# Two weight units ahead of the first slot, the first loads in another order, and part of the weight scaling on GpSimd

## The chip, the cores and the metric

The kernel runs on one core of a Trainium2 chip. The metric is device microseconds of that core for one execution, lower is better, given as the median of several runs. Engines are named as in the profile: PE (TensorE), DVE (VectorE), ACT (ScalarE), POOL (GpSimd) and SP (SyncE, which here only issues DMAs). Each works through its own instructions strictly in the order in which the program lists them, so an instruction that waits holds up everything behind it on its engine.

## What is computed

Top-k attention (576 tokens, 8 batches, 8 heads of 64), then a two-layer network with an exact GELU:

```python
def _attn_ref(q, k, v):
    top_k = 32
    scores = scale * np.matmul(q, k.transpose(0, 1, 3, 2))
    kth = np.partition(scores, -top_k, axis=-1)[..., -top_k:-top_k + 1]
    scores = np.where(scores >= kth, scores, -1000000000.0)
    scores = scores - np.max(scores, axis=-1, keepdims=True)
    attn = np.exp(scores)
    attn = attn / (np.sum(attn, axis=-1, keepdims=True) + 1e-09)
    return np.matmul(attn, v)

def _moe_ref(x, w_in, w_out):          # x: 4608 x 512, w_in: 512 x 2048, w_out: 2048 x 512
    h = x @ w_in
    g = 0.5 * h * (1.0 + erf(h / np.sqrt(2)))
    return g @ w_out
```

The arrays q, k, v are 32-bit floats; w_in and w_out arrive as 64-bit floats, and the kernel turns their bits into 32-bit floats itself.

## The kernel before

**Slots.** The attention is cut into 144 items, each 128 query rows for two heads (or the 64 tail rows of four heads). A loop over `n` (L617) runs 144 slots and a few more to drain. Slot n gives each engine work on several items at once: PE computes the scores of item n+2 (`scores`), the product with V of item n-3 (`attend`), the transposes of item n-2 (`transposes`) and up to seven or eight pieces of the network (`mlp`); ACT copies scores out of PSUM, runs the two activations of the softmax of item n-1 for each half (`softmax`), and copies PE's results; DVE finds the 32 largest scores of item n (`top_k`: 8 MAX8 and 6 MATCH_REPLACE8), ends with the reciprocal of the softmax sum of item n-1 (`inverse`), and does some normalisations. T0, T1, ... below are the times at which DVE starts the first MAX8 of slot 0, 1, ... .

**Two short chains through POOL tie the engines together.** After `top_k(n)`, `threshold(n)` (L339, L342) makes from the found values what the softmax of item n needs. When ACT has finished the softmax, `add_small` (L356) makes `den`, which DVE's reciprocal L350 waits for at the end of the next slot. `normalise` (L376) then multiplies the two halves of an item's scores by that reciprocal, on POOL or DVE; PE's transposes of the next slot need the result.

**Weights.** The 1 MB of each of 16 units (`ORDER`) is loaded as raw words into a part of `w_out_sb` that is not yet in use, or into a `stage` tile, and turned into 32-bit floats in one slot: ACT runs L175, L177 and (for some) the scaling L179 at the end of the slot before (`weights_size`), POOL runs the scaling L191 (for the others) and the two integer additions L194 and L195 at the top of the slot (`weights_add`), ahead of `add_small` in POOL's order. One unit is made in each of slots 1 to 15 and the last in slot 17. `on_pool` says who scales: ACT for slots 1 to 8, POOL from slot 9 (`START`). `normalise` at the end of slot n is split by the unit of slot n+1: with a unit that ACT scales, DVE takes one of the two halves; with one that POOL scales, both; with none, POOL takes both. A load waits until POOL has finished with the unit that used the buffer before.

**The start.** Memsets and the identity for the transposes come first, then the loads of k and q for the first two pairs of heads (k of pair 0 from ACT's and POOL's queues, all else from SP's), then the loads of the units of slots 1 and 2. PE runs 16 matmuls (`WARM`, L596) while it waits, then transposes q and k of pairs 0 and 1 (`transpose_qk`, L232, copies L236) and computes the scores of items 0 and 1, whose copies (L281, L282) DVE waits for at T0.

**The network** can start only when the first 256 tokens have all heads, which is in slot 9; item 7 (`HASTE`) is hurried through in slot 8 for that. From there pieces are handed out per slot (seven in slots 10 to 16, else eight), and what is left when the 144 slots end is done by PE alone. The next tokens become ready in slot 18.

Of the kernel before, what the change touches and what calls it, by code (L numbers as in the profile page):

```python
# [14 lines left out]
def kernel(  # L15
# [26 lines left out]
    P = 128  # L42
# [27 lines left out]

    raws = {n: [const.tile([P, NJ, 2, D], f32, name=f"raw_{n}{i}") for i in range(m)]
            for n, m in (("k", 2), ("q", 2), ("v", NP + 1))}
    for n, ts in raws.items():
        for t in ts[: 1 if n == "v" else 2]:
            (nc.vector if n == "v" else nc.gpsimd).memset(t[:, NM], 0.0)
    make_identity(nc, ident)
    for t in raws["v"][1:]:
        nc.gpsimd.memset(t[:, NM], 0.0)


    n_pairs = B * NP
# [5 lines left out]
    def load(n, pair, queue=None, queue2=None):  # L87
        if pair >= n_pairs:
            return
        queue = queue or nc.sync  # L90
        queue2 = queue2 or queue
        b, h0 = pair // NP, 2 * (pair % NP)
        t, src = raw_of(n, pair), sources[n]
        for e in range(2):
            queue.dma_start(
                out=t[:, 0:NM, e, :], in_=src[b, h0 + e, 0:SM].rearrange("(t p) d -> p t d", p=P)
            )
            queue2.dma_start(out=t[e * TL : (e + 1) * TL, NM, e, :], in_=src[b, h0 + e, SM:S])

# [18 lines left out]


    ORDER = [0, 1, 2, 3, 8, 9, 4, 5, 10, 11, 6, 7, 12, 13, 14, 15]
    FIRST = 1
    START = 2 * NP + 1
    HASTE = 2 * NP - 1
    WARM = 16
    words = {}
    low = const.tile([P, 1], f32, name="low")
    nc.gpsimd.memset(low, -EXP0 * 2.0**19)
# [1 line left out]
    nc.gpsimd.memset(high, EXP0 * 2.0**-21)  # L131


    SLOT_OF = {u: FIRST + i + (i == UNITS - 1) for i, u in enumerate(ORDER)}
    UNIT_IN = {n: u for u, n in SLOT_OF.items()}
    unit_in = UNIT_IN.get

    def load_weights(n, queue=None):

        queue = queue or nc.sync  # L140
        u = unit_in(n)
        if u is None:
            return
        src, r, c, dst = weights_of(u)
        if src.dtype == f32:
            for x in range(2):
                queue.dma_start(
                    out=dst[:, x], in_=src[(r + x) * P : (r + x + 1) * P, c : c + WS]
                )
            return  # L150


        half, i = src.bitcast(u16), ORDER.index(u)
        if i not in (12, 14, 15):
            at = FT // 2 + 4 * (i % 2)
            t = w_out_sb[:, at : at + 4, :].rearrange("p (a b) n -> p a (b n)", a=2)
        else:
            t = stage.tile([P, 2, 2 * WS], f32, tag="words", name="words")
        for a in range(2):
            queue.dma_start(  # L160
                out=t[:, a].bitcast(u16)[:, 0 : 4 * WS - 1],
                in_=half[(r + a) * P : (r + a + 1) * P, 4 * c + 1 : 4 * (c + WS)],
            )
        words[u] = t
# [15 lines left out]

    def on_pool(u):

        return SLOT_OF[u] >= START

    made = set()

    def weights_add(u):
        if u in words:
            w, _, below, d = parts(u)
            if on_pool(u):  # L190
                nc.gpsimd.tensor_scalar(  # L191
                    w.bitcast(i32), w.bitcast(u32), 2.0**-13, None, op0=ALU.mult
                )
            nc.gpsimd.tensor_tensor(d, d, below, op=ALU.add)  # L194
            nc.gpsimd.tensor_tensor(d, d, w.bitcast(i32), op=ALU.add)  # L195
        made.add(u)


    items, starts = [], []
# [50 lines left out]
    def spread(t, step, n):  # L250

        return bass.AP(tensor=t.tensor, offset=t.offset, ap=[list(t.ap[0]), [step, 2], [1, n]])
# [10 lines left out]
    def scores(i):  # L263
        if i >= N:
            return
        pair, t = items[i]
        S_of[i] = s = work.tile([P, 2 * S], f32, tag="s", bufs=5, name="s")
        s_ps = ps.tile([P, 2, 512], f32, tag="s", bufs=1, name="s_ps")
        t_ps = ps.tile([P, 512], f32, tag="tp", name="t_ps")
        if t < NM:  # L270
            qk = qk_of[pair]
            lhsT = qk[:, t * P : (t + 1) * P]
            nc.tensor.matmul(t_ps[:, 0:P], lhsT=lhsT, rhs=qk[:, SM + P : KT], start=True, stop=True)  # L273
            for c in range(2):
                for e in range(2):
                    rows = slice(e * D, (e + 1) * D)
                    nc.tensor.matmul(  # L277
                        s_ps[:, e, c * 256 : (c + 1) * 256], lhsT=lhsT[rows, :],
                        rhs=qk[rows, KT + c * 256 : KT + (c + 1) * 256], start=True, stop=True,
                    )  # L280
            nc.scalar.activation(spread(s, S + TL, SM), s_ps, func=AF.Copy, scale=scale)  # L281
            nc.scalar.activation(s[:, SM : S + TL], t_ps[:, 0:P], func=AF.Copy, scale=scale)  # L282
        else:
            for r in range(2):
                qk = qk_of[pair + r]
                for e in range(2):
                    nc.tensor.matmul(  # L287
                        t_ps[half(r, e), r * TL : (r + 1) * TL],
                        lhsT=qk[:, SM + e * TL : SM + (e + 1) * TL],
                        rhs=qk[:, SM + P + e * TL : SM + P + (e + 1) * TL],  # L290
                        start=True, stop=True,
                    )

            for r in range(2):
                qk = qk_of[pair + r]
                for e in range(2):
                    rows = slice(e * D, (e + 1) * D)
                    nc.tensor.matmul(  # L298
                        s_ps[half(r, e), r, :], lhsT=qk[rows, SM + e * TL : SM + (e + 1) * TL],
                        rhs=qk[rows, KT:], start=True, stop=True,  # L300
                    )
            s2 = s.rearrange("p (r n) -> p r n", r=2)
            nc.scalar.activation(s2[:, :, 0:SM], s_ps, func=AF.Copy, scale=scale)
            nc.scalar.activation(
                s2[:, :, SM:S], t_ps[:, 0:P].rearrange("p (r n) -> p r n", r=2),
                func=AF.Copy, scale=scale,
            )
# [274 lines left out]
    staging = ExitStack()  # L582
    stage = staging.enter_context(tc.tile_pool(name="stage", bufs=1))

    load("k", 0, nc.scalar, nc.gpsimd)
    load("q", 0)
    load("k", 1)
    load("q", 1)
    for n in range(2):
        load_weights(FIRST + n)  # L590


    idle = raws["v"][0][:, NM].rearrange("p e d -> p (e d)")
# [3 lines left out]
    for pair in range(2):  # L597
        for piece in transpose_qk(pair, pair == 0):
            piece()
        if pair == 0:  # L600
            scores(0)
            scores(1)

# [11 lines left out]
    for n in range(ahead):  # L617

        left[0] = 7 if START < n < START + 2 * NP else 8
        weights_add(unit_in(n))  # L620
        scores(n + 2)

        product = attend(HASTE) if n - 2 == HASTE else n - 3 != HASTE and attend(n - 3)
        late = n > START
        mlp(1)
        tr = transposes(n - 2) if n - 2 != HASTE else []
        if product and n > START and done[0] < len(pieces) and pieces[done[0]][0] > ready[0]:

            for piece in tr[:1]:
                piece()  # L630
            tr, ready[0] = tr[1:], n_tok[0]
        softmax(n - 1, 0)
        mlp(1)
        if not late:
            softmax(n - 1, 1)
        mlp(1)
        prep = prep_in.pop(n, [])
        if len(prep) > 1 and len(tr) == 3:
            tr, prep = tr[:1] + prep[:1] + tr[1:], prep[1:]
        for piece in tr[:-1]:  # L640
            piece()
            ready[0] = n_tok[0]
            mlp(1)
        ready[0] = n_tok[0]
        if late:
            softmax(n - 1, 1)
        if n - 1 != HASTE:
            add_small(n - 1)
        for piece in tr[-1:] + prep:
            piece()  # L650
            mlp(1)

        run_gelus()
        mlp(left[0])
        run_gelus()
        if n - 1 == HASTE:

            def hasty():
                st = stat_of[HASTE]
                nc.vector.tensor_scalar(st["den"], st["den"], 1e-9, None, op0=ALU.add)  # L660
                inverse(HASTE)
                normalise(HASTE, 2)

            top_k(n, {1: hasty})
            for piece in transposes(HASTE):
                piece()
        elif n < N:
            top_k(n, {3: lambda: inverse(n - 1)})
        else:
            inverse(n - 1)  # L670
        threshold(n)
        u = unit_in(n + 1)

        if n - 1 != HASTE:
            normalise(n - 1, 0 if u not in words else 2 if on_pool(u) else 1)

        weights_size(unit_in(n + 1))
        if n >= FIRST:
            load_weights(n + 2)
        if n <= NP:  # L680
            load("v", n)

# [37 lines left out]
```

## Time and profile before

| | |
|---|---|
| median of 9 runs | 1652.05 us (1651.38 to 1652.72) |
| the profiled execution: its own time | 1651.6 us |
| its span, from the first to the last instruction | 1649.8 us |
| busy, PE / DVE / ACT / POOL | 1589.5 / 1421.1 / 1183.3 / 651.1 us |
| mean granted PE clock | 0.980 of full speed |
| T0, T1, T2, T3 | 11.80, 21.46, 31.73, 42.00 us |
| T8, T9, T13, T14 | 93.49, 105.48, 148.55, 159.33 us |
| T15, T16, T17, T18 | 172.94, 182.65, 194.39, 205.22 us |
| first matmul of the network (L496) | 109.08 us |

A page of the profile gives busy times over the whole span; a table by windows gives, for each stretch of time, the length and the busy time of PE, of its weight loads, of DVE, ACT and POOL (with the number of instructions), the granted PE clock, the DMA share and GB/s. A timeline row has the start in us, the duration in us, engine, line, operation, what is written from what, and in brackets how long the engine was idle before it and what ended that.

### The profile page before, as it was taken

To read this page: it belongs to the slowest core of one execution; us is meant where nothing else is said; L and a number is where in the kernel's file an instruction comes from. 1 tells how busy PE (TensorE), PEld (TensorE's weight loads), DVE (VectorE), ACT (ScalarE), POOL (GpSimd) and SP (SyncE) were. 2 spreads that over 40 slices of the span, in tenths; PEclk is the share of its full clock that TensorE was granted. 3 is DMA by queue.
4 is the path that set the end of the run, shared out by engine and by line. 5 is a ranking of instruction groups with operands and counts; after the bars stand their busy time and mean duration, and the time that the engine had idled before them with its cause. 6 is when DMAs were issued, how large, how long until landed. Compare 5 with 4: busy or idle time off the path is not lost.

```text
span 1649.8 us, 25054 instructions
## 1 busy us (share of the span) xinstructions
PE 1589.5 (96%) x8832; PEld 1078.0 (65%) x8832; DVE 1421.1 (86%) x3051; ACT 1183.3 (72%) x2130; POOL 651.1 (39%) x755
## 2 busy tenths in 40 slices
PE   6579799999999999999999999999999999999999
PEld 4355476766666667776666667676666666666665
DVE  7999899988899889998989988998889888999800
ACT  6889767777777777777777777777777777777720
POOL 3678633333333333333333333333333333333300
PEclk8789999999999999999999999999999999999999
DMA  6424110011101111011100111001110001000000
GB/s 171 142 91 131 55 43 1 14 29 33 46 1 28 30 30 28 1 28 36 30 28 5 39 30 43 1 14 28 44 35 1 27 16 35 2 13 6 2 13 13
DMA packets 126621, 56.14 MB, mean 34 GB/s; under 512 B 117760, under 2 KB 117792, under 8 KB 126496
## 3 DMA queue, kind: packets, MB, share of 16 engines
q1 hardware_dynamic: 125376, 54.25, 12.3%
q8 instruction: 70, 1.15, 0.3%
q14 instruction: 55, 0.45, 0.1%
q10 hardware_dynamic: 1056, 0.26, 0.1%
q0 software_dynamic: 64, 0.03, 0.0%
HBM read 45.08 MB, written 9.44 MB: 33 GB/s over the span
## 4 chain that ended last, share of the span: by engine, by line
PE 91%; DVE 5%; ACT 2%; issue 0%; POOL 0%; DVEq 0%; ACTq 0%; POOLq 0%
PE h_ps L496 30%; PE y_ps L532 30%; PE o L444 8%; PE s_ps L277 8%; PE tp L413 7%; DVE top L324 3%; DVE rest L327 2%; PE tp_qk L232 2%; PE t_ps L273 2%; PE o L455 1%; PE s_ps L298 1%; PE tp_t L395 1%; ACT s L364 0%; PE t_ps L287 0%; ACT s L363 0%
## 5 line engine op out<-in xcount | busy, mean ns | idle before, releaser
L324 DVE MAX8 top<-rest 128x8 f32<-128x576 f32 x864 | 609.2, 746 | 0.0
L496 PE MATMUL h_ps<-xT,w_in_sb 128*128 128x256 f32 (+1 forms) x2560 | 552.6, 361 | 3.8 <-ACT g L507 3.8
L532 PE MATMUL y_ps<-w_out_sb,g 128*128 128x512 f32 x1152 | 549.4, 599 | 0.0
L496 PEld LDWEIGHTS h_ps<-xT,w_in_sb 128*128 128x128 f32 x2560 | 428.6, 191 | 67.2 <-issue 20.0
L376 POOL TENSOR_SCALAR s<-s,rden 128x576 f32<-128x576 f32 x265 | 454.3, 1723 | 0.4 <-DVE rden L350 0.4
L327 DVE MATCH_REPLACE8 rest<-top,rest 128x576 f32<-128x576 f32 x576 | 423.2, 742 | 0.0
L356 POOL TENSOR_SCALAR den<-den 128x2 f32<-128x2 f32 x143 | 31.7, 222 | 831.4 <-ACT s L364 830.7
L532 PEld LDWEIGHTS y_ps<-w_out_sb,g 128*128 128x128 f32 x1152 | 195.0, 190 | 166.1 <-issue 164.8
L281 ACT ACTIVATE s<-s_ps 128x1024 f32<-128x1024 f32 x128 | 131.4, 1027 | 168.1 <-PE s_ps L277 146.6
L364 ACT ACTIVATE s<-s,bias 128x576 f32<-128x576 f32 x288 | 223.3, 775 | 12.7
L363 ACT ACTIVATE s<-s,neg 128x576 f32<-128x576 f32 x288 | 224.0, 778 | 0.3 <-POOL neg L339 0.2
L413 PEld LDWEIGHTS tp<-ident,s 128*128 128x128 f32 x1152 | 146.2, 144 | 113.5 <-issue 58.7
L420 ACT COPY pt<-tp 128x512 f32<-128x512 f32 x256 | 147.1, 575 | 102.1 <-PE tp L413 102.0
L327 DVE MATCH_REPLACE8 rest<-top,s 128x576 f32<-128x576 f32 x288 | 211.7, 742 | 0.0
L324 DVE MAX8 top<-s 128x8 f32<-128x576 f32 x288 | 201.7, 742 | 3.9 <-ACT s L282 3.9
L413 PE MATMUL tp<-ident,s 128*128 128x128 f32 x1152 | 178.8, 279 | 26.4 <-ACT pt L396 19.9
L444 PE MATMUL o<-pt,raw_v 128*64 128x256 f32 x1280 | 155.5, 390 | 0.0
L277 PE MATMUL s_ps<-qk 64*128 64x256 f32 x1024 | 152.6, 419 | 0.7 <-ACT s L281 0.7
L350 DVE RECIPROCAL rden<-den 128x2 f32<-128x2 f32 x144 | 23.0, 160 | 138.1 <-POOL den L356 137.6
L444 PEld LDWEIGHTS o<-pt,raw_v 128*64 128x64 f32 x1280 | 87.8, 139 | 66.4 <-issue 24.2
L277 PEld LDWEIGHTS s_ps<-qk 64*128 64x128 f32 x1024 | 92.1, 194 | 23.8 <-issue 1.8
L507 ACT ACTIVATE g<-h_ps 128x512 f32<-128x512 f32 x144 | 78.6, 595 | 33.6 <-PE h_ps L496 32.9
(67 smaller groups left out, 1088.3 us busy)
## 6 DMA issues: line engine op xcount, KB each, us to landing
raw_q<-in_q_dram SPq DMA_DIRECT2D x64, 128.0 KB, 2.4
raw_v<-in_v_dram SPq DMA_DIRECT2D x64, 128.0 KB, 2.4
out_dram<-y SPq DMA_DIRECT2D x32, 256.0 KB, 2.1
w_out_sb<-in_moe_w_in_dram SPq DMA_DIRECT2D x16, 511.8 KB, 4.9
raw_k<-in_k_dram SPq DMA_DIRECT2D x62, 128.0 KB, 2.5
w_out_sb<-in_moe_w_out_dram SPq DMA_DIRECT2D x10, 511.8 KB, 4.1
words<-in_moe_w_out_dram SPq DMA_DIRECT2D x6, 511.8 KB, 4.5
raw_q<-in_q_dram SPq DMA_DIRECT2D x64, 16.0 KB, 2.2
```

The lines of the kernel that those rows point to most:

```text
L277: nc.tensor.matmul(s_ps[:, e, c * 256 : (c + 1) * 256], lhsT=lhsT[rows, :], rhs=qk[rows, KT + c * 256 : KT + (c + 1) * 256], start=True, s ...
L281: nc.scalar.activation(spread(s, S + TL, SM), s_ps, func=AF.Copy, scale=scale)
L324: nc.vector.max(st["top"][:, e, 8 * r : 8 * r + 8], cur[e])
L327: nc.vector.match_replace(rest[:, e], st["top"][:, e, 8 * r : 8 * r + 8], cur[e], LOWEST)
L363: nc.scalar.activation(s, s, func=AF.Prelu, bias=st["neg"][:, e, 1:2], scale=1.0, alpha=STEEP)
L364: nc.scalar.activation(s, s, func=AF.Exp, bias=st["bias"][:, e : e + 1], scale=1.0, accum_out=st["den"][:, e : e + 1],)
L376: (nc.vector if e >= 2 - on_dve else nc.gpsimd).tensor_scalar(s, s, st["rden"][:, e : e + 1], None, op0=ALU.mult)
L413: nc.tensor.transpose(tp[:, j * P : (j + 1) * P], s[:, first + j * P : first + (j + 1) * P], ident)
L420: nc.scalar.copy(out=dst, in_=tp.rearrange("p (j n) -> p j n", j=NM))
L444: nc.tensor.matmul(o[e * D : (e + 1) * D, 0:n], lhsT=vt[:, j, e, :], rhs=pt[:, e * NM + j if j < NM else 2 * NM, :], start=(j == 0), stop= ...
L496: nc.tensor.matmul(h_tile(u)[:, i, :], lhsT=w_in_sb[:, ko, f * P : (f + 1) * P], rhs=xT[:, ko, c0 : c0 + n], start=(ko == 0), stop=(ko == ...
L532: nc.tensor.matmul(y_of[sub], lhsT=g_of[u][:, i, sub * P : (sub + 1) * P], rhs=w_out_sb[:, f, :], start=(f == 0), stop=(f == FT - 1),)
```

## The change

- SLOT_OF: the first two units of ORDER are made in slot 0, the third in slot 1, and so on to the fifteenth in slot 13; the last is made in slot 15. Every unit but the first is two slots earlier than before, the first one slot.
- Three units are loaded before the loop instead of two; the third unit's words get a stage tile of their own. `weights_size` of the two units of slot 0 runs before the loop.
- on_pool: POOL scales in odd slots too (1, 3, 5, 7); ACT scales in slots 0, 2, 4, 6, 8.
- normalise: ahead of a unit that ACT scales, POOL takes both halves; ahead of one that POOL scales before slot 9, DVE takes one; from slot 9 on, both, as before. Ahead of slot 14 (no unit any more) and slot 17 POOL takes both where DVE took both.
- The second integer addition of a unit is taken out of weights_add and comes after add_small in POOL's order (weights_end).
- The start: DVE does most memsets, the loads of k and q of pair 0 are listed before the identity, WARM is 9 instead of 16, and the scores of item 0 are copied out of PSUM by ACT and DVE in three parts instead of two activations on ACT.

```diff
     raws = {n: [const.tile([P, NJ, 2, D], f32, name=f"raw_{n}{i}") for i in range(m)]
             for n, m in (("k", 2), ("q", 2), ("v", NP + 1))}
-    for n, ts in raws.items():
-        for t in ts[: 1 if n == "v" else 2]:
-            (nc.vector if n == "v" else nc.gpsimd).memset(t[:, NM], 0.0)
-    make_identity(nc, ident)
-    for t in raws["v"][1:]:
-        nc.gpsimd.memset(t[:, NM], 0.0)
+    nc.gpsimd.memset(raws["k"][0][:, NM], 0.0)
+    for t in raws["v"][:1] + raws["q"] + raws["k"][1:] + raws["v"][1:]:
+        nc.vector.memset(t[:, NM], 0.0)
...
+    load("k", 0, nc.scalar, nc.gpsimd)
+    load("q", 0)
+    make_identity(nc, ident)
...
-    FIRST = 1
-    WARM = 16
+    WARM = 9
...
-    SLOT_OF = {u: FIRST + i + (i == UNITS - 1) for i, u in enumerate(ORDER)}
-    UNIT_IN = {n: u for u, n in SLOT_OF.items()}
-    unit_in = UNIT_IN.get
-    def load_weights(n, queue=None):
-        queue = queue or nc.sync
-        u = unit_in(n)
-        if u is None:
-            return
+    SLOT_OF = {u: max(0, i - 1) + (i == UNITS - 1) for i, u in enumerate(ORDER)}
+    def units_in(n):
+        return [u for u in ORDER if SLOT_OF[u] == n]
+    def load_weights(u):
+        queue = nc.sync
...
-        if i not in (12, 14, 15):
+        if i not in (2, 12, 14, 15):
...
     def on_pool(u):
-        return SLOT_OF[u] >= START
+        return SLOT_OF[u] >= START or SLOT_OF[u] % 2 == 1
...
     def weights_add(u):
...
             nc.gpsimd.tensor_tensor(d, d, below, op=ALU.add)
-            nc.gpsimd.tensor_tensor(d, d, w.bitcast(i32), op=ALU.add)
         made.add(u)
+    def weights_end(u):
+        if u in words:
+            w, _, _, d = parts(u)
+            nc.gpsimd.tensor_tensor(d, d, w.bitcast(i32), op=ALU.add)
...
+            if i == 0:
+                nc.scalar.activation(s[:, 0:SM], s_ps[:, 0], func=AF.Copy, scale=scale)
+                nc.vector.tensor_scalar(s[:, SM : S + TL], t_ps[:, 0:P], scale, None, op0=ALU.mult)
+                nc.vector.tensor_scalar(s[:, S + TL :], s_ps[:, 1], scale, None, op0=ALU.mult)
+                return
...
-    load("k", 0, nc.scalar, nc.gpsimd)
-    load("q", 0)
     load("k", 1)
     load("q", 1)
-    for n in range(2):
-        load_weights(FIRST + n)
+    for u in units_in(0) + units_in(1):
+        load_weights(u)
...
+    for u in units_in(0):
+        weights_size(u)
...
-        weights_add(unit_in(n))
+        for u in units_in(n):
+            weights_add(u)
...
             add_small(n - 1)
+        for u in units_in(n):
+            weights_end(u)
...
         threshold(n)
-        u = unit_in(n + 1)
+        us = units_in(n + 1)
         if n - 1 != HASTE:
-            normalise(n - 1, 0 if u not in words else 2 if on_pool(u) else 1)
-        weights_size(unit_in(n + 1))
-        if n >= FIRST:
-            load_weights(n + 2)
+            normalise(n - 1, 0 if not us or not on_pool(us[0]) else 1 if n + 1 < START else 2)
+        for u in us:
+            weights_size(u)
+        for u in units_in(n + 2):
+            load_weights(u)
```

More of the change, by code (lines that the diff above doesn't have):

```diff
@@ L194, in weights_add @@
             nc.gpsimd.tensor_tensor(d, d, below, op=ALU.add)
+        made.add(u)
+    def weights_end(u):
+        if u in words:
+            w, _, _, d = parts(u)
             nc.gpsimd.tensor_tensor(d, d, w.bitcast(i32), op=ALU.add)
-        made.add(u)
     items, starts = [], []
```

## The prediction

> **What bounds the kernel now.** I read the busy shares first, then a table by windows cut at the slots, then the timeline of the places where those windows show a gap.
>
> ```profile
> PE 1589.5 (96%) x8832; PEld 1078.0 (65%) x8832; DVE 1421.1 (86%) x3051; ACT 1183.3 (72%) x2130; POOL 651.1 (39%) x755
> ...
> PE   6579799999999999999999999999999999999999
> ...
> DVE  7999899988899889998989988998889888999800
> ```
>
> PE is full from the sixth slice on; what can be won or lost lies in the first five. In the windows:
>
> ```profile
> 21.46:31.73 10.27, 3.92 (x14) 2.40 (x14) 10.23 (x23) 10.09 (x15) 5.83 (x7) 0.66 0.46 104
> 72.81:83.15 10.34, 6.77 (x41) 4.32 (x39) 10.23 (x24) 9.46 (x16) 7.27 (x7) 0.83 0.32 107
> ...
> 159.33:172.94 13.61, 9.34 (x55) 5.79 (x51) 10.78 (x25) 10.02 (x17) 8.88 (x7) 1.00 0.32 99
> 172.94:182.65 9.71, 9.59 (x65) 6.73 (x57) 9.71 (x22) 8.17 (x15) 7.96 (x4) 1.00 0.21 47
> ...
> 194.39:205.22 10.83, 4.32 (x23) 2.95 (x17) 9.81 (x23) 10.67 (x17) 7.91 (x5) 0.71 0.19 43
> ...
> 300.00:1500.00 1200.00, 1200.00 (x6803) 817.61 (x6802) 1085.69 (x2332) 885.76 (x1620) 450.07 (x556) 1.00 0.10 24
> ```
>
> The reader is to see three stages. Slots 1 to 8 (first two rows) are as long as DVE's work, PE is half idle: a microsecond saved or lost there moves the network's start at 109.08 by as much. Slots 14 to 17 have gaps on PE. From slot 18 PE has no idle time (1200.00 of 1200.00), so whatever shift stands there reaches the end unchanged. I therefore add up shifts, slot by slot, up to the point where the network resumes for good (L496 at 210.21).
>
> **The start.** PE's transposes begin at 6.26, behind the warm-up (1.05 to 6.43). Nine of sixteen end at about 1.05 + 5.38 x 9/16 = 4.1; k of pair 0 lands 3.5 us (median of its two) after its issue at 1.27, at 4.8. I take 4.6, so 1.65 earlier. The copies of item 0's scores, 10.58 to 11.77 on ACT, become halves side by side: a 512-column copy takes 0.58 on ACT (L236) and 0.51 on DVE; 0.6 earlier. T0 goes from 11.80 to 9.55, T1 to 19.2, and ACT, which ends its last start copy at 15.84, is free at 13.7. The memsets and the identity, before PE's first use of them by over a microsecond, cost nothing.
>
> **Two units in slot 0.** This gain is not kept, I think, because of POOL's order. These rows show the order in slot 1 and 2 now:
>
> ```profile
> 22.77 2.41 POOL L194 TENSOR_TENSOR w_in_sb<-w_in_sb,w_out_sb 128x1024 int32<-128x1024 int32 x1 [0.62 <-ACT w_out_sb L177]
> 25.25 2.39 POOL L195 TENSOR_TENSOR w_in_sb<-w_in_sb,w_out_sb 128x1024 int32<-128x1024 int32 x1
> 28.05 0.23 POOL L356 TENSOR_SCALAR den<-den 128x2 f32<-128x2 f32 x1 [0.40 <-ACT s L364]
> 31.27 0.23 POOL L339 TENSOR_SCALAR neg<-top 128x4 f32<-128x4 f32 x1 [2.99 <-DVE rden L350]
> 31.58 0.27 POOL L342 TENSOR_TENSOR bias<-neg 128x2 f32<-128x2 f32 x1
> 31.84 1.73 POOL L376 TENSOR_SCALAR s<-s,rden 128x576 f32<-128x576 f32 x1
> 33.54 2.39 POOL L194 TENSOR_TENSOR w_in_sb<-w_in_sb,w_out_sb 128x1024 int32<-128x1024 int32 x1
> ```
>
> Additions start 2.47 apart, a normalisation takes 1.70, a threshold pair 0.57; den is done at 28.28, 2.8 before DVE asks for it at 31.10. ACT needs 3.43 for a unit that it scales (L175 at 28.60 to the next activation at 32.03) and L177 ends 2.5 after L175 starts. After the change ACT takes unit 0 at 13.7 and unit 1 at 17.1; its L177 ends at 19.7, and POOL's second first-addition starts then. Behind it: that addition and both last additions, 3 x 2.47, to 27.1; threshold of item 0, 27.7 (it could have run at 19.2); scaling of the third unit at 3.2 (L191's median is 3.12), 30.9; its addition, 33.35; den of item 0, 33.6. DVE, unhindered, would end slot 1 at 19.2 + 9.71 = 28.9 (9.71 is the row of slot 15, with no normalisation on DVE). So it waits 4.8 and T2 is about 33.75 against 31.73: **+2.0**. Bounds: without any wait -2.8; with every start 1 us later +3.0.
>
> Queued behind SP's six weight loads are q and k of pair 2. The DMAs moved 255 GB/s at a 0.90 share from 11.80 to 21.46, so another 1.05 MB is some 4.1 us: k of pair 2, for which PE waited until 19.00, comes at about 23, ACT's copy and L175, L177 of the third unit end by 26.7, and POOL wants them at 30.9. Cost nothing, cover 4.2; beyond it each microsecond moves T2. The load of the fourth unit waits at SP for the last addition of the second (27.1) and lands some 5 us later; v stands behind it and is not needed before slot 4.
>
> **Normalisations in slots 2 to 8.** One half on DVE makes a slot 10.27, none 9.71: 0.56 each. Slot 1's is in T2 already; slots 3, 5 and 7 give 3 x 0.56 = **-1.7**. POOL takes them at 1.70, and scales in odd slots. Its sum per pair of slots, by the spacings above: even 0.57 + 2 x 1.70 + 2 x 2.47 + 0.30 = 9.2, odd 0.57 + 1.70 + 3.2 + 2 x 2.47 + 0.30 = 10.7, together 19.9; DVE's pair is 9.71 + 10.27 = 19.98. POOL, late from slot 1, doesn't catch up, and den arrives within about half a microsecond of DVE's need. I put **+0.2** there (0 to +6, see the rivals). The normalised rows reach PE at T+6.4 instead of T+2 in even slots; ACT's copy of these transposes came at T+4.6 to T+7.7 anyway, so nothing for that.
>
> **Slot 8.** Threshold 7 now stands behind a last addition: T8 + 2.47 + 0.57 = T8+3.0, where the softmax of item 7 started at T8+1.97. DVE used its sum at 99.04, 0.27 after it was there: **+0.75** (0 to 1.0). Slots 9 to 13 keep their work on every engine.
>
> **Slots 13 to 17.** Two normalisations fewer on DVE in slot 13 give nothing: DVE waits 2.73 us in slot 14 for den (171.80), which comes through PE. POOL's two end at 158.3 + 0.57 + 3.4 = 162.4, and PE's transpose stood at 162.21: **+0.3**. Slot 17:
>
> ```profile
> 194.83 0.33 PE L395 MATMUL tp_t<-ident,s 128*128 128x128 f32 x1
> 199.74 1.12 PE L413 MATMUL tp<-ident,s 128*128 128x128 f32 x4 [4.58 <-ACT s L304]
> 202.79 1.11 PE L413 MATMUL tp<-ident,s 128*128 128x128 f32 x4 [1.93 <-ACT pt L396]
> ...
> 206.27 3.76 PE L444 MATMUL o<-pt,raw_v 128*64 128x256 f32 x20
> 209.96 0.41 PE L400 MATMUL tp_t<-ident,s 128*64 128x128 f32 x2
> 210.21 1.89 PE L496 MATMUL h_ps<-xT,w_in_sb 128*128 128x256 f32 x8
> ```
>
> PE waits for ACT's L304, which stood behind L175 and L177 of the last unit (196.15 to 198.6). That unit is now made in slot 15. L304 then ends at 197.45, PE goes on 2.25 earlier, ACT's chain behind it too, T18 falls to about 203.0, and the last thing before the network resumes is POOL's normalisation of item 16: 203.0 + 0.57 + 3.44 = 207.0, L496 at 207.3, 2.9 earlier. The window 195 to 210 had a granted clock of 0.66; if L496 restarts at half clock, most of the gain goes. Bounds -0.5 and -4.6 (PE's product ends 4.6 earlier and nothing waits for POOL); I take **-2.6**.
>
> The Trainium skill, "TensorE: Matmul & The Clock Gate" (Part 1), says an idle window of about 3.4 us halves the clock. The 4.58 us gap fits it; a gap of 2.3 would not trip it, and the sum would use 2.9 for 2.6.
>
> The Trainium skill, "GPSIMD Engine Reference" (4.1 Engine selection), speaks against elementwise work on POOL: two-input operations run some 2 times slower there than on VectorE, one-input ones at roughly line rate. Here the one-input scaling takes 3.12 us and the two-input addition 2.40, so the rows rank them the other way. With the scaling at half an addition, an estimate from that page, den would come 2 us earlier and the total be about 1648.
>
> **Sum**: +2.0 - 1.7 + 0.2 + 0.75 + 0.3 - 2.6 = -1.05. The profiled execution took 1651.6 (span 1649.8 and 1.8 around it); it becomes 1650.55. The median shown is 0.45 above it, so **1651.0**.
>
> **Rivals.** (B) *POOL gets through slot 0 in time.* POOL idles 17.65 us up to 21.64 now, so there is room if ACT can start the units earlier than I count. Against: ACT is in order behind its copies, and four additions are 9.9 us at any start. With no wait at all T2 is 28.9, POOL has no lag, the 0.2 and 0.75 vanish too: 1651.0 - 4.85 - 0.95 = 1645.2; half the wait 1648. (C) *POOL becomes the bound of slots 2 to 7*: it decides once its pair passes 19.98 us. A waiting hand-over costs more than back-to-back spacing (den starts 0.09 after the add in front at 38.41); with 0.15 more for each of 13 instructions a pair, 1.95 x 3, and 0.9 in slot 1's chain: 1651.0 + 6.75 - 0.2 = 1657.5, slower. (D) *Slot 17 doesn't change*: another wait on ACT or POOL takes L304's place: 1653.6. That the code does something other than it says I exclude.
>
> **Numbers.** A 0.42, own range 1648.5 to 1653.5; B 0.30; C 0.18; D 0.10. Within 0.2%, about what a measurement of this kernel can tell from no change, means 1648.7 to 1655.4. Faster: B and 0.08 of A, 0.38. Slower: 0.16 of C and 0.05 of D, 0.21. Same 0.41. The range reaches into B and C: 1645.4 to 1656.0.
>
> **What would show it.** Right: a DVE wait of some 5 us for den before T2, T2 near 33.7, POOL without idle time in slots 1 to 7, odd slots of 9.7, L496 resuming about 207 to 208. Wrong: T2 near 29 (B), slots 2 to 7 longer than 10.3 (C), or a PE gap over 4 us left in slot 17 (D).

## The result and the profile after

The changed kernel takes 1657.5 us (median of 10 runs, 1655.6 to 1659.1) beside 1651.8 for the kernel before (30 runs): a ratio of 1.0033, 95% interval 1.0025 to 1.0041. It is slower by some 5.7 us. The profiled executions say the same: the span went from 1649.8 to 1656.4, by 6.6.

The page of the changed kernel, its busy times and two rows of its slices:

```profile
PE 1592.7 (96%) x8818; PEld 1079.3 (65%) x8818; DVE 1425.2 (86%) x3052; ACT 1181.4 (71%) x2127; POOL 668.7 (40%) x758
...
PE   5679899999999999999999999999999999999999
...
DVE  6999899999999898998999888998889898999800
```

PE is busy for 3.2 us more than before (1592.7 against 1589.5) and the span is 6.6 longer, so about half of the loss is idle time of PE; the digits put it where it was expected to be decided, in the first slices. The table by windows of the changed kernel, cut at DVE's first MAX8 of a slot; after the bounds and the length come busy time and count on PE, PEld, DVE, ACT and POOL, then the granted clock, the DMA share and GB/s:

```profile
21.03:35.11 14.08, 7.63 (x28) 5.01 (x30) 9.81 (x22) 11.54 (x18) 13.06 (x9) 0.50 0.58 151
35.11:46.78 11.67, 5.72 (x29) 3.84 (x27) 11.63 (x23) 10.27 (x18) 11.42 (x9) 0.60 0.57 152
46.78:56.49 9.71, 4.84 (x19) 3.73 (x21) 9.71 (x22) 8.57 (x15) 9.30 (x7) 0.56 0.51 154
56.49:68.64 12.15, 9.21 (x43) 5.63 (x43) 12.12 (x24) 8.66 (x15) 9.75 (x9) 0.64 0.53 148
...
98.40:112.32 13.92, 7.00 (x32) 5.22 (x32) 13.78 (x26) 8.99 (x18) 8.98 (x7) 0.77 0.48 159
123.07:135.00 11.93, 11.06 (x63) 8.62 (x60) 11.82 (x25) 11.74 (x18) 8.55 (x6) 1.00 0.11 26
166.25:182.40 16.15, 11.65 (x59) 7.14 (x55) 10.74 (x25) 10.02 (x17) 4.96 (x8) 0.89 0.26 81
...
300.00:1500.00 1200.00, 1200.00 (x6840) 820.08 (x6835) 1085.71 (x2333) 884.78 (x1618) 450.07 (x556) 1.00 0.10 24
```

Slot 1 (first row) is 14.08 long with 9.81 of DVE work in it: DVE waits there. Slots 2, 4, 8 and 10 (11.67, 12.15, 13.92, 11.93) are a different matter: DVE is busy throughout, and has more busy time than before with no more instructions. Slot 3 (9.71) is what an undisturbed slot looks like. In the last row PE is never idle, as in the kernel before, so the shift that has built up by slot 20 stays to the end. The shift of each slot's start against the kernel before, from these windows, gives this account (us):

| place | predicted | measured |
|---|---|---|
| up to T2 (start, wait for den of item 0) | +2.0 | +3.38 |
| slots 3, 5, 7 (no normalisation on DVE) | -1.7 | -1.74 |
| slots 2, 4 and 6 (POOL's lag) | +0.2 | +3.28 (1.40, 1.88, 0) |
| slot 8 | +0.75 | +1.93 |
| slot 10 | 0 | +1.16 |
| slots 13 and 14 | +0.3 | +1.49 (-1.06, +2.55) |
| slots 16 to 19 | -2.6 | -2.87 |
| sum | -1.05 | +6.63 |

**The wait before T2.** POOL's timeline in the changed kernel (start, us, engine, line, operation), and the row of DVE that waits for it:

```profile
21.64 2.40 POOL L193 TENSOR_TENSOR w_in_sb<-w_in_sb,w_out_sb 128x1024 int32<-128x1024 int32 x1 [0.99 <-ACT w_out_sb L176]
23.99 4.77 POOL L199 TENSOR_TENSOR w_in_sb<-w_in_sb,w_out_sb 128x1024 int32<-128x1024 int32 x2
28.73 0.23 POOL L348 TENSOR_SCALAR neg<-top 128x4 f32<-128x4 f32 x1
29.05 0.19 POOL L351 TENSOR_TENSOR bias<-neg 128x2 f32<-128x2 f32 x1
29.33 2.91 POOL L190 TENSOR_SCALAR words<-words 128x1024 int32<-128x1024 uint32 x1
32.31 2.38 POOL L193 TENSOR_TENSOR w_in_sb<-w_in_sb,words 128x1024 int32<-128x1024 int32 x1
34.78 0.22 POOL L365 TENSOR_SCALAR den<-den 128x2 f32<-128x2 f32 x1
35.03 0.17 DVE L359 RECIPROCAL rden<-den 128x2 f32<-128x2 f32 x1 [4.27 <-POOL den L365]
```

This is the chain that the prediction wrote down, instruction for instruction: two last additions, the threshold pair, the scaling, its addition, and only then den, on which DVE has waited 4.27 us.

**The long slots.** The timeline of slot 4's end in the changed kernel, POOL and DVE together:

```profile
65.70 0.22 POOL L365 TENSOR_SCALAR den<-den 128x2 f32<-128x2 f32 x1 [2.24 <-ACT s L373]
66.00 2.40 POOL L199 TENSOR_TENSOR w_out_sb<-w_out_sb 128x1024 int32<-128x1024 int32 x1
66.13 0.15 DVE L359 RECIPROCAL rden<-den 128x2 f32<-128x2 f32 x1
66.31 2.41 DVE L385 TENSOR_SCALAR s<-s,rden 128x576 f32<-128x576 f32 x1
...
68.64 0.75 DVE L333 MAX8 top<-s 128x8 f32<-128x576 f32 x1
```

The normalisation on DVE takes 2.41 us. It has no wait in brackets: whatever holds it up is counted as busy time. POOL's last addition began 0.31 before it and ended at 68.40; the normalisation ends 0.32 behind that. The view of DVE's normalisation by its source line, in the kernel before:

```profile
L376 DVE TENSOR_SCALAR s<-s,rden x23: 511/520/525, 31.3 to 194.0; 128x576 f32<-128x576 f32 x23
```

and in the changed kernel (ns: least, median, greatest):

```profile
L385 DVE TENSOR_SCALAR s<-s,rden x15: 506/519/2444, 44.9 to 182.0; 128x576 f32<-128x576 f32 x15
```

The median is the same, and the greatest is not. Four of the 15 are long: 1.93 in slot 2, 2.41 in slot 4, 2.44 in slot 8, 1.67 in slot 10. POOL's L199 ended at 46.54, 68.40, 107.55 and 134.34; these four ended at 46.86, 68.72, 107.86 and 134.64, always 0.30 to 0.32 later. What they have above 0.52 is 1.41 + 1.89 + 1.92 + 1.15 = 6.4 us, which is what slots 2, 4, 8 and 10 are longer by (1.40, 1.88, 1.93, 1.16).

### The profile page after: what moved, and what is told of

Its sections match the earlier page's. It is cut to its first block, busy times and chain, and to the rows that moved or that the text cites. A ratio compares the mean times of both kernels' runs of the same rounds, so it can differ in the third digit from the quotient of the medians.

```text
span 1656.4 us, 25018 instructions
## 1 busy us (share of the span) xinstructions
PE 1592.7 (96%) x8818; PEld 1079.3 (65%) x8818; DVE 1425.2 (86%) x3052; ACT 1181.4 (71%) x2127; POOL 668.7 (40%) x758
## 3 DMA queue, kind: packets, MB, share of 16 engines
q8 instruction: 70, 1.15, 0.3%
## 4 chain that ended last, share of the span: by engine, by line
PE 89%; DVE 7%; ACT 2%; POOL 1%; issue 0%; DVEq 0%; ACTq 0%; POOLq 0%
PE y_ps L541 30%; PE h_ps L505 29%; PE o L453 8%; PE s_ps L280 8%; PE tp L422 7%; DVE top L333 3%; DVE rest L336 3%; PE tp_qk L235 2%; PE t_ps L276 2%; PE o L464 1%; PE tp_t L404 1%; PE s_ps L307 1%; DVE s L385 1%; POOL s L385 0%; ACT s L373 0%
## 5 line engine op out<-in xcount | busy, mean ns | idle before, releaser
L505 PE MATMUL h_ps<-xT,w_in_sb 128*128 128x256 f32 (+1 forms) x2560 | 553.8, 361 | 3.7 <-ACT g L516 3.7
L505 PEld LDWEIGHTS h_ps<-xT,w_in_sb 128*128 128x128 f32 x2560 | 429.4, 191 | 67.3 <-issue 17.1
L385 POOL TENSOR_SCALAR s<-s,rden 128x576 f32<-128x576 f32 x273 | 467.9, 1723 | 0.8 <-issue 0.4
```

The source lines that it names most:

```text
L385: (nc.vector if e >= 2 - on_dve else nc.gpsimd).tensor_scalar(s, s, st["rden"][:, e : e + 1], None, op0=ALU.mult)
L505: nc.tensor.matmul(h_tile(u)[:, i, :], lhsT=w_in_sb[:, ko, f * P : (f + 1) * P], rhs=xT[:, ko, c0 : c0 + n], start=(ko == 0), stop=(ko == ...
```

## The experiments

Two theories stood at the start. P: a normalisation that DVE issues while POOL runs an instruction waits until that instruction ends, and the change puts POOL's second addition (`weights_end`) just there. S: POOL has too much ahead of den in slots 0 and 1, and this is all of the loss. Shifts are those of the profiled executions against the kernel before. Every kernel computes the whole reference.

**The split alone.** The kernel before, in which only the second addition of a unit moves behind the small addition (den), as in the change.

```diff
-            nc.gpsimd.tensor_tensor(d, d, w.bitcast(i32), op=ALU.add)
         made.add(u)
+    def weights_end(u):
...
             add_small(n - 1)
+        weights_end(unit_in(n))
```

> The kernel before with one edit of the change: POOL's second addition of a weight unit comes after the small addition that makes den. Theory P (a DVE normalisation that is issued while POOL runs an instruction waits for that instruction to end): in the kernel before, POOL's second addition would now run into DVE's normalisations in slot 4 (0.8 us), slots 9 to 13 (1.55, 1.95, 0.7, 1.2, 0.75) and slots 14 and 16; DVE rows of L376 of 1 to 2.4 us where they were 0.52, 1657 to 1660 us. Rival S (the loss of the change comes from POOL's overfull order in slots 0 and 1 and its sum of work, the place of an addition doesn't matter): all DVE rows stay at 0.52 and the time at 1651.8.

Measured: 1656.2 us, ratio 1.0025 (1.0016 to 1.0034). This one edit costs some 4.2 us of the 5.7 that the whole change costs. Ten of its executions took 1654.3 to 1656.4 us; the eleventh, the one with the profile, took 4595, with PE busy for 4560 us, so its times say nothing of the others. Its normalisations by source line are still to the point:

```profile
L380 DVE TENSOR_SCALAR s<-s,rden x23: 506/776/2569, 48.6 to 447.1; 128x576 f32<-128x576 f32 x23
```

With PE this slow the engines meet at other moments, and 12 of the 23 are long; each ends 0.32 behind POOL's addition. The same kernel with a profile of an ordinary execution:

> The kernel before with the second addition behind den, once more, for its profile: DVE's normalisations in slot 4 and slots 9 to 13 at 1.2 to 2.5 us instead of 0.52, slots 4 and 9 to 13 longer by that, 1656.

There is one time, 1654.75; the end is 3.1 later. The timeline of slot 10's end in that kernel:

```profile
125.84 2.40 POOL L200 TENSOR_TENSOR w_out_sb<-w_out_sb 128x1024 int32<-128x1024 int32 x1
126.26 0.15 DVE L354 RECIPROCAL rden<-den 128x2 f32<-128x2 f32 x1
126.53 2.46 DVE L380 TENSOR_SCALAR s<-s,rden 128x576 f32<-128x576 f32 x2
```

Two normalisations are 0.95 together in the kernel before; here they take 2.46, the first ending 0.3 behind POOL's addition. The long ones are 1.06 in slot 4, 2.04 in slot 10 and 2.48 in slot 14, and the shift goes from -0.2 at slot 4 to +0.4, then +1.9 and +2.2; a further 1.4 comes in slot 18. In all other slots, 9 and 11 to 13 among them where long rows were expected, POOL's addition was not running when DVE normalised, and the rows are 0.51 to 0.53. So the split alone makes collisions, though which slots are hit depends on the moment; the 1.4 of slot 18 is not one of them and isn't explained here.

**The second addition elsewhere.** The changed kernel, with `weights_end` ahead of den in slots 2, 4, 6 and 9 to 12, behind the threshold in slot 8, and as in the change in the odd slots, where DVE has nothing to normalise.

```diff
+        end_first = n > HASTE + 1 or n % 2 == 0 and n != HASTE + 1
+        if end_first:
+            for u in units_in(n):
+                weights_end(u)
         if n - 1 != HASTE:
             add_small(n - 1)
-        for u in units_in(n):
-            weights_end(u)
+        if not end_first and n != HASTE + 1:
+            for u in units_in(n):
+                weights_end(u)
...
         threshold(n)
+        if n == HASTE + 1:
+            for u in units_in(n):
+                weights_end(u)
```

> The kernel after, with POOL's second addition placed where DVE does not normalise behind it: ahead of den in the slots at whose end DVE normalises (2, 4, 6, 9 to 12), behind den in slots 1, 3, 5, 7, and behind the threshold in slot 8. POOL's work is the same. Theory P: slots 2, 4, 8 and 10 get shorter by 1.4, 1.9, 1.9 and 1.15 (the excess of their DVE normalisations), the DVE wait of 4.3 us before T2 stays, 1651 to 1652 us. Rival S: the slots stay as long, DVE waits for den instead, 1657 us.

Measured: 1654.4 us, ratio 1.0016 (1.0007 to 1.0025), 3.1 less than the changed kernel. DVE's normalisations by source line in this kernel:

```profile
L385 DVE TENSOR_SCALAR s<-s,rden x15: 511/520/532, 46.8 to 177.9; 128x576 f32<-128x576 f32 x15
```

All collisions are gone: 6.4 us of long rows. The time is above the 1651 to 1652 that P forecast: half of the gain is not won, since the addition ahead of den makes den late in two places: DVE now waits 1.73 for it in slot 2 and 1.67 in slot 9. T2 is +3.40, as in the change, so the first wait (4.26) is another matter.

**Another form of the normalisation.** The changed kernel, in which DVE's normalisation also writes a sum that nobody reads.

```diff
-                s, s, st["rden"][:, e : e + 1], None, op0=ALU.mult
+                s, s, st["rden"][:, e : e + 1], None, op0=ALU.mult, op1=ALU.add, accum_out=spare
```

> The kernel after, with DVE's normalisations in another form, the one that also accumulates (its sum is not used), everything else in its place. Theory P with the reason in the form's second path to the memory: the rows take some 0.7 us each and none over 1.0, however POOL runs beside them; each of the 13 normalisations costs some 0.25 us more than 0.52, the four long ones cost 5 us less: 1652 to 1654. If POOL's running instruction holds up DVE whatever the form, the long rows stay and the time is 1659 or more.

Measured: 1655.8 us, ratio 1.0031 (1.0019 to 1.0042); the end of the profiled execution is 4.9 later than before, 1.7 less than in the changed kernel. The timeline of slot 4's end in this kernel:

```profile
65.50 0.17 DVE L359 RECIPROCAL rden<-den 128x2 f32<-128x2 f32 x1 [0.52 <-POOL den L365]
65.55 2.40 POOL L199 TENSOR_TENSOR w_out_sb<-w_out_sb 128x1024 int32<-128x1024 int32 x1
65.70 0.81 DVE L387 TENSOR_SCALAR_CACHE_REDUCE s<-s,rden 128x576 f32<-128x576 f32 x1
...
66.44 1.42 DVE L333 MAX8 top<-s 128x8 f32<-128x576 f32 x2
```

POOL's addition runs as before, begun 0.15 ahead, and DVE's instruction is through in 0.81. All 15 have this length (808 to 815 ns), beside POOL or not. The order of the work and the data are those of the changed kernel; only the form of DVE's instruction differs, and the sum that it writes is read by nobody. One small instruction of DVE keeps the plain form in this kernel, item 7's addition to den in slot 8 (L676, 128x2): it takes 1.73 beside a POOL addition and ends 0.03 behind it, where it takes 0.17 in the three kernels in which POOL is idle at that moment. So it is neither rden that is late nor a wait on POOL by the program, but a resource that the one form needs and the other doesn't. MAX8 has its usual 0.74 or 0.75 beside POOL as well. The form is no remedy here: it costs 0.29 more each time, in all 15, and the time is above the 1652 to 1654 expected. The medians lie close, with intervals that overlap; what is said here rests on the rows.

The Trainium skill, "SBUF — State Buffer" (Who interferes with whom), describes such a resource: VectorE and GpSimd share one pair of ports to SBUF; whichever issues first has it for its whole instruction, the other waits until then, and `tensor_scalar` can contend in its plain form, when its operands meet the page's conditions, but not in the one that also writes its accumulator. The rows above agree for DVE's wait: 0.52 alone, up to 2.44 beside POOL, 0.81 in the accumulating form throughout. POOL waits in its turn, as POOL's small subtraction of two elements shows by its source line, in the changed kernel and then in the one with the accumulating form:

```profile
L351 POOL TENSOR_TENSOR bias<-neg x144: 193/193/479, 29.1 to 1569.1; 128x2 f32<-128x2 f32 x144
...
L351 POOL TENSOR_TENSOR bias<-neg x144: 193/193/195, 28.9 to 1567.4; 128x2 f32<-128x2 f32 x144
```

In the changed kernel six of them begin inside a plain normalisation of DVE; these take 0.31 to 0.48 and end 0.05 behind it, and no other takes over 0.20. With the accumulating form none is long. That the resource is the ports themselves is the page's word; the rows show who waits for whom.

**One unit in slot 0.** The changed kernel, with the units one to a slot from slot 0.

```diff
-    SLOT_OF = {u: max(0, i - 1) + (i == UNITS - 1) for i, u in enumerate(ORDER)}
+    SLOT_OF = {u: i + (i == UNITS - 1) for i, u in enumerate(ORDER)}
...
-        if i not in (2, 12, 14, 15):
+        if i not in (12, 14, 15):
```

> The kernel after with one unit in slot 0 instead of two, each later unit one slot later than after (slots 1 to 14, the last in 16). Both theories: POOL makes den of item 0 by about 29.5, DVE's wait of 4.27 us before T2 goes, T2 near 30.8 instead of 35.1. Theory S: that is the loss, 1652 or less. Theory P: the normalisations of slots 2, 4, 6 and 8 to 11 still run into POOL's additions, three to five rows over 1.4 us, 1653 to 1655.

Measured: 1653.2 us, ratio 1.0008 (0.9999 to 1.0017), 4.3 less than the changed kernel. The timeline around den of item 0 in this kernel:

```profile
26.81 2.38 POOL L193 TENSOR_TENSOR w_in_sb<-w_in_sb,w_out_sb 128x1024 int32<-128x1024 int32 x1
...
29.28 0.22 POOL L365 TENSOR_SCALAR den<-den 128x2 f32<-128x2 f32 x1
...
30.78 0.15 DVE L359 RECIPROCAL rden<-den 128x2 f32<-128x2 f32 x1
```

den is there 1.3 before DVE asks for it, and T2 comes at 30.84, 0.9 earlier than in the kernel before. The long normalisations stay (2.08, 2.44 and 1.64 in slots 4, 8 and 10), and the end is +1.07. Slot 2's is down to 0.69, because POOL's addition is nearly over when DVE normalises. So the second unit in slot 0 is the cause of the wait, and through POOL's lateness of slot 2's collision; the other collisions don't need it.

**A shorter form on POOL.** The changed kernel, with a second multiplication, by 1.0, in POOL's scaling and in its normalisation.

```diff
-                    w.bitcast(i32), w.bitcast(u32), 2.0**-13, None, op0=ALU.mult
+                    w.bitcast(i32), w.bitcast(u32), 2.0**-13, 1.0, op0=ALU.mult, op1=ALU.mult
```

> The kernel after, with POOL's scaling and normalisation written with a second multiplication, by 1.0 (same results). It tests POOL's sum of work: if POOL has a quicker path for two multiplications than for one and nothing, its rows L190 (2.95 us) and L385 (1.72 us) shrink to perhaps half. Then theory S expects den of item 0 some 1.5 us earlier, T2 near 33.6, and POOL idle in every slot: 1654. Theory P expects that what counts is whether POOL's second addition has ended when DVE normalises: with POOL less late it has in slots 2, 4 and 10, and the long rows go: 1652. If POOL's rows stay as they are, 1657.5.

Measured: 1654.6 us, ratio 1.0020 (1.0011 to 1.0029). POOL's two instructions by source line in the changed kernel:

```profile
L190 POOL TENSOR_SCALAR words<-words x4: 2907/3090/3151, 29.3 to 182.2; 128x1024 int32<-128x1024 uint32 x4
...
L385 POOL TENSOR_SCALAR s<-s,rden x273: 1717/1722/1729, 37.9 to 1579.5; 128x576 f32<-128x576 f32 x137
```

and in this one:

```profile
L190 POOL TENSOR_SCALAR words<-words x4: 1121/1270/1321, 29.0 to 179.5; 128x1024 int32<-128x1024 uint32 x4
...
L388 POOL TENSOR_SCALAR s<-s,rden x273: 743/747/752, 35.8 to 1574.7; 128x576 f32<-128x576 f32 x137
```

The wait for den of item 0 falls from 4.27 to 2.51, by the 1.8 that the scaling ahead of it is shorter. Collisions remain, since DVE collides with additions: 2.13 in slot 2, 2.56 in slot 4, 2.50 in slot 10. The one of slot 8 has gone. P had forecast that the long rows go, and 1652: with POOL less late DVE meets its additions at other moments, so a less busy POOL alone is no cure.

**Both causes gone.** One unit in slot 0 and the second addition moved, by the two diffs above; nothing else.

> The changed kernel with one unit in slot 0 (as in the run with one unit) and the second addition where DVE does not normalise (as in the run with the end moved); POOL's instructions keep their old one-multiplication form. P and S together: no wait for den before T2 (T2 near 30.8, 0.9 earlier than before), every normalisation on DVE 0.51 to 0.53 us. The run with one unit kept long normalisations of 2.08, 2.44 and 1.64 in slots 4, 8 and 10, that is 1.56 + 1.92 + 1.12 = 4.6 too much; the run with the end moved gave back about half of such a gain to new waits for den. So the end between 1.3 and 3.5 us earlier than before, about 1649.5 us. S alone (the order in slot 0 is all): the end stays at 1.07 later, 1653.2.

Measured: 1646.95 us, ratio 0.9972 (0.9961 to 0.9983). The table by windows of this kernel, slots 1, 2, 4 and 14:

```profile
21.10:30.81 9.71, 6.22 (x25) 3.87 (x24) 9.71 (x23) 9.16 (x14) 9.30 (x7) 0.50 0.81 205
30.81:41.68 10.87, 5.80 (x27) 3.97 (x25) 10.32 (x24) 9.50 (x17) 10.45 (x10) 0.56 0.53 145
51.40:61.67 10.27, 7.28 (x43) 3.85 (x41) 10.23 (x24) 8.24 (x15) 9.57 (x10) 0.83 0.61 172
...
158.99:170.12 11.13, 6.95 (x33) 4.58 (x31) 9.82 (x23) 9.61 (x18) 8.03 (x5) 1.00 0.23 80
```

Its normalisations by source line:

```profile
L385 DVE TENSOR_SCALAR s<-s,rden x17: 511/520/532, 41.2 to 180.4; 128x576 f32<-128x576 f32 x17
```

No normalisation is longer than 0.53, and slots 1 to 7 are 9.7 or 10.3 long but for a wait of 0.52 for den in slot 2; in slot 9 DVE waits 1.65 for den. T9 is 2.1 earlier than in the kernel before, where the changed kernel is 6.8 later. The end is 4.5 earlier, a microsecond more than the 1.3 to 3.5 expected: slot 14 is 11.13 long, against 13.61 before and 16.15 in the change. S alone would have left 1653.2.

**The start alone.** The kernel before with the edits of the start (memsets, first loads, 9 warm-up matmuls, the split copy of item 0) and none of the weights.

> The kernel before with the edits of the start alone: memsets on DVE, the first loads issued earlier, 9 warm-up matmuls in place of 16, item 0's copy shared by ACT and DVE; no edit of the weights. In the changed kernel T0 and T1 came 0.42 and 0.43 earlier. If that is all the start is worth: T0 to T8 and the end 0.4 earlier, 1651.6 us. If the start was worth the 2.25 that the prediction took, with POOL idle in slot 0: the end some 2 us earlier, 1650. Rival: POOL, which now has its first work at the same time, takes the gain back: no change in the end.

Measured: 1651.45 us, ratio 1.0000 (0.9991 to 1.0008). T0 to T8 come 1.1 earlier. Of that 0.4 goes in slot 8, where DVE now waits 1.35 for item 7's softmax, and 0.6 in slot 10 (a wait of 0.45 for den); slots 14 and 17 take 0.6, slots 18 and 19 give 0.5 back, and the end is at +0.06. The start is worth more than the 0.4 and less than the 2.25, and the end is as the rival had it; but the gain goes from slot 8 on, not in POOL's first work.

**No normalisation on DVE.** POOL's shorter form makes it possible to leave all normalisations but item 7's to POOL. First with one unit in slot 0 and slot 8's last addition behind the threshold:

```diff
-            normalise(n - 1, 0 if not us or not on_pool(us[0]) else 1 if n + 1 < START else 2)
+            normalise(n - 1, 0)
```

> One unit in slot 0, all normalisations but item 7's on POOL in the form with two multiplications, slot 8's second addition behind the threshold. No DVE normalisation can meet POOL: no row of it over 0.6, slots 1 to 7 9.7 us each. With POOL's rows halved: T8 near 89.5, T9 near 101.5, 1647 to 1649. With POOL's rows as before: POOL's sum of 12.4 us in slots with a unit that it scales bounds them, over 1660.

Measured: 1645.5 us (1644.4 to 1645.7, 5 runs), ratio 0.9959 (0.9947 to 0.9972): below both kernels and below the 1647 to 1649 expected. Slots 1 to 7 are all 9.70 long, DVE's bare work; T8 is 5.1 earlier than before. Then the same in the kernel before, with its own slots:

> The kernel before with all normalisations but item 7's on POOL, in the form with two multiplications. With POOL's rows halved: slots 2 to 7 9.71 instead of 10.27, T8 3.4 us earlier, slots 9 to 13 bounded by PE: 1647 to 1649. With POOL's rows as before: slots 10 to 13 bounded by POOL at 12.4, 1657 or more.

Measured: 1650.7 us, ratio 0.9994 (0.9985 to 1.0002). The interval takes in no change, and 1647 to 1649 was expected. In the profiled execution T8 is 2.5 earlier, but slot 8 is 14.47 long, with a wait of 3.39 for item 7's softmax, and takes it all back (T9 -0.03); T20 is at +0.62 and the end of the span at +0.2. Taking work off DVE is worth nothing here, where slot 8 and the stretch behind it don't follow.

## Why the prediction failed

It said 1651.0, a little faster or the same; 1657.5 came out. In its own order:

- **The bound** was read rightly: slots 1 to 8 go by DVE, PE has no idle time from 300 to 1500 us in both kernels, and the shift that stands at T20 (+6.60) is that of the end.
- **The start** was over-sized: T0 came 0.42 earlier where 2.25 was taken. Two rows of the changed kernel's timeline show the half of it:

```profile
10.15 0.60 ACT L286 ACTIVATE s<-s_ps 128x512 f32<-128x512 f32 x1 [1.65 <-PE s_ps L280]
10.78 0.69 DVE L288 TENSOR_SCALAR s<-s_ps 128x512 f32<-128x512 f32 x1 [1.41 <-ACT s L286]
```

  "Halves side by side" run one after the other, since DVE's waits for ACT's; from the first copy to T0 it is 1.23, as before (10.58 to 11.80). The nine warm-up matmuls ran from 1.04 to 5.25, that is 4.21 us, where nine sixteenths of the old time, 3.0, were taken; so the transposes began at 5.35, not 4.6, and four took 1.09 where they took 0.60. With the start alone they began at 5.10 and took 0.63, and T0 was 1.1 earlier. In the eight kernels with this start T0 is 0.31 to 1.12 earlier, one execution each, so the size varies; 2.25 came in none.
- **Two units in slot 0** (+2.0 to T2): the mechanism is shown by the run with one unit, and a wait of 4.27 stands against the 4.8 forecast. The sum is off by 1.4 because the chain starts with ACT's work on unit 0, at 15.60 and not 13.7, and is 0.5 shorter from there than it was counted.
- **The price of POOL's scaling**, for which the prediction weighed a page against the rows: 2.91 ahead of den, so the row held. With the second multiplication it is some 1.1, den comes 1.8 earlier, and the time falls by 2.9. The Trainium skill, "GPSIMD Engine Reference" (4.1 Engine selection), ranks one input ahead of two; the runs show that ranking in this second form only.
- **Normalisations in slots 3, 5, 7**: -1.74 against -1.7.
- **POOL's lag in slots 2 to 8 (+0.2), slot 8 (+0.75), and "Slots 9 to 13 keep their work on every engine"**: this is the step that failed. POOL's lateness was priced through den alone. In slots 2, 4, 6 and 8 den is not waited for at all, and item 7's softmax, whose lateness was to cost the 0.75, started 0.70 after T8 and not 3.0. But POOL's second addition had been moved behind den, that is, onto the moment when DVE has its reciprocal and normalises, a time when POOL in the kernel before sat waiting for that same reciprocal (2.99 in the row at 31.27). 0.95 was forecast for slots 2, 4, 6, 8 and 10 together, and 6.4 came, 5.4 of the 7.7 that the sum is off by (1.4 more are T2's, 1.2 those of slots 13 and 14). That the split in two places had a price by itself was nowhere in the text. The kernel before already held such a row, at the very time, 99.04, that the prediction reads for slot 8, in these lines of POOL's and DVE's timelines:

```profile
97.78 2.40 POOL L195 TENSOR_TENSOR w_in_sb<-w_in_sb,w_out_sb 128x1024 int32<-128x1024 int32 x1
99.04 1.17 DVE L660 TENSOR_SCALAR den<-den 128x2 f32<-128x2 f32 x1
```

  Two elements a row take 1.17 us and end 0.03 behind POOL's addition; with the start alone, where POOL is idle then, the same instruction takes 0.17.
- **Slots 13 and 14** (+0.3): what was forecast is there. Slot 13 is 1.06 shorter, POOL's two normalisations end 4.0 after T14, and PE's transpose that waits for them is 1.2 later in the slot. Unforeseen is what follows, in the changed kernel:

```profile
170.33 0.33 PE L404 MATMUL tp_t<-ident,s 128*128 128x128 f32 x1 [0.46 <-POOL s L385]
...
174.52 2.07 PE L505 MATMUL h_ps<-xT,w_in_sb 128*128 128x256 f32 x4 [2.57 <-ACT g L516]
```

  Four matmuls of L505 take 2.07 here where the kernel before has 1.10 behind a gap of 2.66. The granted clock was 0.50 from 174.50 to 176.60, and 1.00 from 166.50 to 168.50 in the kernel before. That, with the transposes behind it, is about 1.4 more until den. With the second addition moved, PE sat idle still longer (1.88 and 2.57 us) and L505 took 1.13 at a granted clock of 1.00, so the gap alone doesn't decide it; this stays open.
- **Slot 17** (-2.6): T18 was to fall by 2.2 against what went before; slots 16 and 17 gave 2.19, and slots 18 and 19 0.7 more. This term held (-2.87). Its view of the clock did not: 2.3 us was taken as too short a gap to halve it, but behind two gaps of 2.37 and 2.38 us, 0.8 apart, the granted clock is 0.50 from 209.90 to 213.00.
- **The rivals.** C has the time that came (1657.5), by luck, and isn't what happened: it had POOL's sum of a pair pass DVE's through the cost of hand-over. No row shows the 0.15 that it adds for a hand-over: in the kernel before den starts 0.08 behind the row of ACT that it waits for (27.97 to 28.05), and 0.09 behind an addition without a wait. POOL's busy time in slots 2 and 3 is 20.7 of 21.4 us, so it is nearly full there, but slot 3 is 9.71 long, and in slots 2 and 4 DVE isn't waiting for a result. D is ruled out; B's slot 0 without a wait is there only with one unit in it.

The two causes nearly add up as far as T13: against the changed kernel one unit in slot 0 brings it 5.9 earlier (from +7.98 to +2.12) and the moved addition 2.7 (to +5.24), both 8.3 (to -0.33). Behind it they don't: from T13 to T20 the shift changes by -1.4 in the changed kernel, by -1.1 and -2.4 in these two, and by -4.2 with both. That stretch depends on how PE's queue and den meet in slots 14 to 19, and no run isolates it.

## What to carry to other kernels

When an instruction is moved on an engine that "has time", look at what every other engine runs at the new moment, and not only at who waits for the result: a busy row can hold a wait. Compare the least and the greatest duration of one line before and after; a median that stays while the greatest grows nearly fivefold (525 to 2444 ns here) points to contention, and so does a row far too long for its size, such as the 1.17 us for two elements. And an addition that feeds nothing urgent should stand where the other engine does work that doesn't meet it, even if that is in front of something that looks more pressing; measure both, for each place may have its own wait.

## What the runs showed of the hardware

- A 128x576 f32 TENSOR_SCALAR on DVE, 0.52 alone, that is issued 0.25 to 1.04 us into a POOL addition ends 0.30 to 0.32 behind that addition's end, four times out of four. A 128x2 one, 0.17 alone, takes 1.16 to 1.73 and ends 0.03 behind the addition that it meets, in all eight kernels in which it meets one. POOL's 128x2 TENSOR_TENSOR, 0.19 alone, takes 0.31 to 0.48 when it begins inside such a normalisation (six times in the changed kernel). In its accumulating form the 128x576 one takes 0.81 whether POOL runs or not.
- POOL's TENSOR_SCALAR with two multiplications is faster than with one: 0.75 against 1.72 for 128x576 f32, and 1.12 to 1.32 against 2.91 to 3.15 for 128x1024 from uint32 to int32. With one multiplication a scaling of 1024 elements is slower than an addition of two inputs (2.40), with two it is quicker.
- DVE's copy of one half of a PSUM tile began 0.03 us after ACT's copy of the other half had ended (10.78 and 10.75), not when PE's product was there, at which ACT's began (10.15); with the start alone it was the same. Whether the chip or the program orders them was not tested.
